# Backward input-gradient product: most x rows ride in the memory rows' column groups, the rest once per four segments

## The chip, the cores and the metric

The kernel runs on one core of one Trainium2 chip. The metric is the time of one execution in microseconds (us) on the device. Each ratio below is made among executions that took turns on the same chip. The times of the backward chain, the waits and the clocks are read from one profiled execution of each kernel, and not all of these ran on the same chip; the changed kernel was profiled twice, on two chips, and its chain took 1388.1 and 1385.1 us. Ratios and profiles here are of executions in the state "fast".

Names of engines in the profile: PE is TensorE (matrix products), PEld its weight loads, DVE is VectorE, ACT is ScalarE, POOL is GpSimd, SP is SyncE (here it only issues DMAs). A name with a q at its end (SPq, ACTq) is the time in that engine's instruction queue. "PEclk" is the clock that the chip granted to TensorE, as a share of full speed.

## The reference, cut to what matters

One transformer-like block with a recurrent memory, and its gradients. The sequence of 2048 rows is cut into 64 segments of 32 rows. Each segment attends to its own 32 rows and to 8 memory rows, and the 8 memory rows that leave it enter the next one:

```python
for s in range(n_seg):                      # 64 segments, one after the other
    xs = x[:, s * seg_len:(s + 1) * seg_len, :]
    h = jnp.concatenate([mem, xs], axis=1)  # 8 memory rows + 32 x rows = 40
    q, k, v = h @ Wq, h @ Wk, h @ Wv        # 16 heads of 256 = 4096 columns; the model is 448 wide
    p = softmax(where(mask, q @ k.T * scale, -1e9))
    o = (p @ v) @ Wo
    mem = o[:, :M, :]                       # goes into the next segment
    outs.append(o[:, M:, :])
# ... around it: layer norm, residual, a gated feed-forward block
_out, _vjp = jax.vjp(_f, A_x, A_mem0, A_Wq, ...)
_grads = _vjp(grad_out)
```

The gradient runs through the segments in the opposite order: segment s needs the gradient of its outgoing memory from segment s + 1. This chain of 64 dependent steps can't be parallelised.

## The kernel before

The program has a forward part and the feed-forward block (to about 1810 us), the backward chain of 64 segments (1810 to 3051 us) and a tail with the weight gradients and the x gradient (to 3886 us). One step of the backward chain, cut:

```python
for s in range(NSEG - 1, -1, -1):
    t, r = divmod(s, 4)                      # group of four segments, place in it (3, 2, 1, 0)
    ...
    with k.prio.crit():
        pss = [k.ps1() for _ in range(3)]
        for j in range(MC):                  # MC = 32: the Wo product, 128 matmuls -> doT
            ...
        for b in range(3):
            c0, n, v = c12(pss[b], b)
            k.evac(doT[:, c0:c0 + n, 0:L], v, "vsv"[b])        # PSUM -> SBUF on DVE (v) or ACT (s)
        nc.sync.dma_start_transpose(out=dO_sb, in_=doT...)     # "the doT transfer": v needs it
        pD = k.ps1()
        ...                                  # softmax backward on DVE -> dS_bd; 16 transposes on PE -> dST_bd
        for wi, (nm, lhs, rhs, WT) in enumerate((("k", Q_sb, dS_bd, WkT_sb), ("v", dO_sb, P_bd, WvT_sb),
                                                 ("q", K_sb, dST_bd, WqT_sb))):
            pp = [k.ps1() for _ in range(3)]
            head_mm(pp, lhs, rhs)            # 16 matmuls
            for b in range(3):               # first the 8 memory rows, small evictions
                c0, n, v = c12(pp[b], b)
                k.evac(d8[nm][:, c0:c0 + n, :], v[:, :, SEG:L], "vsv"[b])
            for b in range(3):               # then the 32 x rows, into the block of the group
                c0, n, v = c12(pp[b], b)
                k.evac(blk[nm][:, c0:c0 + n, r * SEG:(r + 1) * SEG], v[:, :, 0:SEG], "svs"[b])
            for j in range(MC):              # gradient of the memory rows: 8 wide, four column groups
                nc.tensor.matmul(pH[32 * (j % 4):32 * (j % 4) + M, 0:D], lhsT=d8[nm][:, j, :], rhs=WT[:, cj(j), :], ...)
        nc.vector.tensor_copy(out=om[:, 0:224], in_=pH[:, 0:224])        # "the omb copy"
        ...                                  # fp32 products with sel add up the four groups -> do_roll of segment s - 1
    ...
    if r == 0:                               # once per four segments, not in the critical chain
        px = k.fx1()
        for wi, (nm, WT) in enumerate((("k", WkT_sb), ("v", WvT_sb), ("q", WqT_sb))):
            for j in range(MC):              # gradient of 128 x rows: 96 matmuls, full width
                nc.tensor.matmul(px[:, 0:D], lhsT=blk[nm][:, j, :], rhs=WT[:, cj(j), :], ...)
            nc.gpsimd.dma_start(out=dr["X_" + nm][t], in_=blk[nm]...)    # 1 MB each: "the X writes"
        ...
```

A scheduler orders the instructions of each engine. What stands in the block of critical priority goes first; the 96 full-width products of a group, "the x products", fill what is left.

## Time and profile before

| | |
|---|---|
| time, median of three runs | 3879.49 us (3871.59 to 3894.95) |
| until the first omb copy | 1810.1 us |
| backward chain, first to last omb copy | 1241.3 us, PEclk 0.95 |
| tail | 835.0 us |
| mean segment in the chain, r = 3 / 2 / 1 / 0 | 23.7 / 18.5 / 17.9 / 19.0 us |

The segment times are the distances of the omb copies in the timeline of DVE, sorted by the place r of the segment in its group of four. The chain runs down, so r = 3 is the first segment after a group's end, when the three X writes are under way; it is called the boundary segment below.

The first part of the profile's page gives the busy time of each engine with its share of the span, here of the kernel before:

```profile
PE 3278.9 (84%) x54326; PEld 2060.7 (53%) x54326; DVE 1366.1 (35%) x3034; ACT 811.9 (21%) x1893; POOL 597.4 (15%) x1253
```

The view by windows cuts the span, here at the first and the last omb copy: the backward chain, then the tail. Its header names the columns.

```profile
core 0: us, PE busy (x) PEld busy (x) DVE busy (x) ACT busy (x) POOL busy (x), PEclk, DMA share, GB/s
1810.10:3051.39 1241.29, 1118.92 (x22044) 716.70 (x22045) 468.48 (x1198) 269.46 (x770) 251.41 (x559) 0.95 0.84 168
3051.39:3886.40 835.01, 718.32 (x3839) 331.63 (x3837) 129.61 (x265) 95.99 (x138) 58.68 (x79) 0.93 0.69 171
```

PE is 90% busy in the chain (1118.9 of 1241.3 us), but that doesn't yet say that its work is what the chain waits for. The chain of waits does: it is followed back from the last instruction, and each line is a start, a duration and what ran or was waited for. One plain segment of the kernel before (arA, arB and arW are three areas of SBUF, the on-chip memory that holds the operands; psf, po and fx are tiles in PSUM, to which the products are written and from which an "eviction" copies them to SBUF; psf L724 is the Wo product, psf L703 are the head products, po L765 the memory rows' products):

```profile
2147.64 3.33 PE psf L724 x128
...
2151.55 4.62 DMA arA<-arA
...
2156.21 0.32 PE psf L703 x4
2156.52 1.62 PE po L765 x32
2158.14 0.54 PE psf L703 x12
2158.68 1.68 PE po L765 x32
```

The longest link of the segment is no product: it is the transfer of doT, 4.62 us. The k branch does not need it. Its softmax backward, head products and evictions ran during the transfer and are not on the chain. Only its 32 memory-row products, the first x32, still follow the transfer, because in PE's queue they stand behind the first 4 head products of v.

Where do the x products run? The groups view (line, engine, operation, output<-input, shape and count; then busy us and mean ns; then idle time before) has their sum, and the timeline of PE (start, duration, count) their places:

```profile
L792 PE MATMUL fx<-arW,arA 128*128 128x448 bf16 x1536 | 370.6, 366 | 13.8 <-issue 13.8
L765 PE MATMUL po<-arW,arB 128*8 128x448 bf16 x6144 | 345.2, 368 | 19.9 <-DMA arW<-in_A_Wv_dram 11.1
```

```profile
2151.91 2.44 PE L792 MATMUL fx<-arW,arA 128*128 128x448 bf16 x12
...
2162.65 0.74 PE L792 MATMUL fx<-arW,arA 128*128 128x448 bf16 x3
...
3053.17 28.93 PE L792 MATMUL fx<-arW,arA 128*128 128x448 bf16 x152
```

Twelve run in the wait for the transfer (2151.55 to 2156.17), some more in the wait for the omb copies at the end of the segment, and 152 are left over when the chain has ended. They come one per 190 ns (28.93 us for 152), while 32 of the 8-wide ones on four column groups take 1.62 to 1.68 us, 52 ns each. That agrees with the Trainium skill, "TensorE: Matmul & The Clock Gate", Part 3: products whose outputs lie in different column groups run in the array at the same time.

### The profile page before, as it was taken

To read this page: it belongs to the slowest core of one execution; us is meant where nothing else is said; L and a number is where in the kernel's file an instruction comes from. 1 tells how busy PE (TensorE), PEld (TensorE's weight loads), DVE (VectorE), ACT (ScalarE), POOL (GpSimd) and SP (SyncE) were. 2 spreads that over 40 slices of the span, in tenths; PEclk is the share of its full clock that TensorE was granted. 3 is DMA by queue.
4 is the path that set the end of the run, shared out by engine and by line. 5 is a ranking of instruction groups with operands and counts; after the bars stand their busy time and mean duration, and the time that the engine had idled before them with its cause. 6 is when DMAs were issued, how large, how long until landed. Compare 5 with 4: busy or idle time off the path is not lost.

```text
span 3886.4 us, 120434 instructions
## 1 busy us (share of the span) xinstructions
PE 3278.9 (84%) x54326; PEld 2060.7 (53%) x54326; DVE 1366.1 (35%) x3034; ACT 811.9 (21%) x1893; POOL 597.4 (15%) x1253
## 2 busy tenths in 40 slices
PE   3888898899888668864898898899999967888899
PEld 2666666666665445643555555556556533333444
DVE  3443344334333346652333343334333232101101
ACT  1222222222222122321221222122222101111200
POOL 3111111111111111121221122112222111000000
PEclk9999999999998789986998999999999988999999
DMA  7444544554544677799798888878888978788652
GB/s 251 143 148 146 174 150 151 162 163 144 168 145 146 167 167 182 180 216 199 167 189 149 158 166 169 165 159 167 177 187 164 306 207 171 142 153 161 163 184 70
DMA packets 1156246, 658.10 MB, mean 169 GB/s; under 512 B 1045268, under 2 KB 1075780, under 8 KB 1148180
## 3 DMA queue, kind: packets, MB, share of 16 engines
q1 hardware_dynamic: 1068100, 392.72, 49.1%
q0 software_dynamic: 60272, 234.11, 17.8%
q10 hardware_dynamic: 27360, 23.58, 2.1%
q8 instruction: 425, 6.96, 0.8%
q14 instruction: 89, 0.73, 0.1%
HBM read 120.04 MB, written 268.02 MB: 100 GB/s over the span
## 4 chain that ended last, share of the span: by engine, by line
PE 64%; DMA 19%; issue 5%; DVE 4%; SPq 4%; ACT 3%; POOL 1%; ACTq 0%; DVEq 0%; POOLq 0%
PE psf L381 11%; DMA arA<-arA 10%; PE po L765 8%; PE psf L875 7%; PE psf L724 5%; PE fx L792 5%; PE po L465 4%; PE psf L703 3%; PE psf L562 2%; PE psf L422 2%; PE fx L494 2%; PE fx L362 2%; PE fx L880 2%; ACT arA L77 2%; PE psf L474 1%
## 5 line engine op out<-in xcount | busy, mean ns | idle before, releaser
L75 DVE CAST arA<-psf 128x480 bf16<-128x480 f32 (+4 forms) x709 | 403.1, 575 | 936.7 <-PE psf L381 323.5
L77 ACT CAST arA<-psf 128x384 bf16<-128x384 f32 (+4 forms) x883 | 404.8, 489 | 1325.5 <-PE psf L381 343.4
L381 PEld LDWEIGHTS <-arW 128*128 128x128 bf16 x16384 | 437.4, 98 | 32.4 <-issue 20.6
L381 PE MATMUL psf<-arA,arW 128*128 128x40 bf16 x16384 | 439.4, 182 | 17.2 <-issue 11.6
L792 PE MATMUL fx<-arW,arA 128*128 128x448 bf16 x1536 | 370.6, 366 | 13.8 <-issue 13.8
L75 DVE CAST arB<-psf 128x96 bf16<-128x96 f32 (+2 forms) x640 | 179.4, 287 | 525.7 <-PE psf L703 284.7
L765 PE MATMUL po<-arW,arB 128*8 128x448 bf16 x6144 | 345.2, 368 | 19.9 <-DMA arW<-in_A_Wv_dram 11.1
L77 ACT CAST arB<-psf 128x96 bf16<-128x96 f32 (+1 forms) x384 | 115.2, 300 | 735.7 <-PE psf L703 566.7
L875 PE MATMUL psf<-arW,arA 128*128 128x512 bf16 x990 | 260.1, 391 | 9.7 <-ACT arA L77 9.7
L724 PE MATMUL psf<-arA,arW 128*128 128x40 bf16 x8192 | 220.4, 180 | 49.7 <-POOL arA L671 38.4
L724 PEld LDWEIGHTS <-arW 128*128 128x128 bf16 x8192 | 219.1, 96 | 69.7 <-issue 55.5
L875 PEld LDWEIGHTS <-arA 128*128 128x128 bf16 x1440 | 138.5, 101 | 212.3 <-issue 73.9
L562 PE MATMUL psf<-arA,arW 128*128 128x256 bf16 x1344 | 167.3, 287 | 79.2 <-DMA arA<-arA 39.1
L765 PEld LDWEIGHTS <-arB 128*8 128x8 bf16 x6144 | 135.8, 88 | 161.3 <-issue 39.2
L792 PEld LDWEIGHTS <-arA 128*128 128x128 bf16 x1536 | 143.5, 106 | 135.6 <-issue 53.0
L562 PEld LDWEIGHTS <-arW 128*128 128x128 bf16 x1344 | 138.1, 103 | 110.6 <-issue 84.7
L362 PE MATMUL fx<-arW,arA 128*128 128x512 bf16 x512 | 136.0, 387 | 52.9 <-DMA arA<-XN 39.4
L422 PE MATMUL psf<-arW,arB 128*32 128x512 bf16 x2048 | 151.1, 387 | 1.8 <-issue 1.8
L465 PE MATMUL po<-arW,arB 128*8 128x448 bf16 x2048 | 146.2, 441 | 2.9 <-DVE arB L75 0.3
L896 PE MATMUL psf<-arW 128*128 128x448 bf16 x450 | 98.8, 371 | 38.8 <-DVE arA L75 38.8
L456 PE MATMUL psf<-arB,arA 128*128 128x80 bf16 x1024 | 53.4, 211 | 90.3 <-DMA arA<-arA 74.6
L703 PE MATMUL psf<-arB,arA 128*128 128x80 bf16 x1024 | 61.4, 212 | 70.3 <-DMA arA<-arA 70.0
(344 smaller groups left out, 3788.9 us busy)
## 6 DMA issues: line engine op xcount, KB each, us to landing
QT<-arA POOLq DMA_DIRECT2D x64, 512.0 KB, 4.0
KT<-arA SPq DMA_DIRECT2D x64, 512.0 KB
VG<-arA SPq DMA_DIRECT2D x64, 512.0 KB
X_o<-arA POOLq DMA_DIRECT2D x40, 512.0 KB, 4.4
Vx<-arA POOLq DMA_DIRECT2D x32, 512.0 KB, 3.3
arA<-Vx SPq DMA_DIRECT2D x128, 128.0 KB
X_k<-arA POOLq DMA_DIRECT2D x16, 1024.0 KB, 7.9
X_v<-arA POOLq DMA_DIRECT2D x16, 1024.0 KB, 8.3
```

The costliest lines, as they stand in the source:

```text
L75: nc.vector.tensor_copy(out=out, in_=in_)
L77: nc.scalar.copy(out=out, in_=in_)
L362: nc.tensor.matmul(pv[:, 0:512], lhsT=hx_b[t % 2][:, kc, :], rhs=Wv_sb[:, kc, n * 512:(n + 1) * 512], start=(kc == 0), stop=(kc == KC - 1))
L381: nc.tensor.matmul(pss[b][:, jj * L:(jj + 1) * L], lhsT=W_sb[:, kc, c * P:(c + 1) * P], rhs=hT_roll[:, kc, sl, :], start=(kc == 0), stop=( ...
L422: nc.tensor.matmul(pV[b][32 * j:32 * j + 32, 0:512], lhsT=memT_pad[:, kc, :], rhs=Wv_sb[:, kc, n * 512:(n + 1) * 512], start=(kc == 0), st ...
L465: nc.tensor.matmul(pO[32 * (j % 4):32 * (j % 4) + M, 0:D], lhsT=o8[:, j, :], rhs=Wo_sb[:, cj(j), :], start=(j < 4), stop=(j >= MC - 4), sk ...
L562: nc.tensor.matmul(ps[:, f2 * 256:(f2 + 1) * 256], lhsT=Wt[:, kc, c * P:(c + 1) * P], rhs=xT[:, kc, :], start=(kc == 0), stop=(kc == KC - 1))
L703: nc.tensor.matmul(ps[b][:, i * 2 * L:(i + 1) * 2 * L], lhsT=lhs[:, cl, :], rhs=rhs_bd[:, cl // 2, :, :].rearrange("p g n -> p (g n)"), st ...
L724: nc.tensor.matmul(pss[b][:, jj * L:(jj + 1) * L], lhsT=WoT_sb[:, kc, c * P:(c + 1) * P], rhs=do_roll[:, kc, sl, :], start=(kc == 0), stop ...
L765: nc.tensor.matmul(pH[32 * (j % 4):32 * (j % 4) + M, 0:D], lhsT=d8[nm][:, j, :], rhs=WT[:, cj(j), :], start=(wi == 0 and j < 4), stop=(wi ...
L792: nc.tensor.matmul(px[:, 0:D], lhsT=blk[nm][:, j, :], rhs=WT[:, cj(j), :], start=(wi == 0 and j == 0), stop=(wi == 2 and j == MC - 1))
L875: nc.tensor.matmul(pa[2 * kc + g][:, 0:w], lhsT=lhs_of(b)[:, kc * P:(kc + 1) * P], rhs=rhs_of(b, g), start=(b == 0), stop=(b == nblk - 1), ...
```

## The change

Its intent: 1536 full-width x products leave the kernel. The memory rows' products use 8 columns of a column group that could take 32, at no more streaming time. So the 40 rows of a segment are put in another order, and 24 of the 32 x rows ride with the 8 memory rows in the same product. Only 8 x rows per segment are left. They are collected over four segments and go, 32 columns in four column groups, through 96 packed products per group. The diff, cut to its core:

```diff
-            pss = [k.ps1() for _ in range(3)]
+            pss = [k.ps1() for _ in range(4)]
 ...
-            nc.sync.dma_start_transpose(out=dO_sb, in_=doT.rearrange("p c n -> p (c n)"))
+            for hf in range(2):                        # two half transposes
+                nc.sync.dma_start_transpose(out=dO_sb[:, 8 * hf:8 * hf + 8, :],
+                                            in_=doT[:, 16 * hf:16 * hf + 16, :].rearrange("p c n -> p (c n)"))
 ... softmax backward: scale fused in, one multiplication into dS_bd instead of two
-            for wi, (nm, lhs, rhs, WT) in enumerate((("k", Q_sb, dS_bd, WkT_sb), ("v", dO_sb, P_bd, WvT_sb),
+            pH = k.po1()
+            for wi, (nm, lhs, rhs, WT) in enumerate((("v", dO_sb, P_bd, WvT_sb), ("k", Q_sb, dS_bd, WkT_sb),
                                                      ("q", K_sb, dST_bd, WqT_sb))):
+                if nm == "k":                          # the 16 transposes into dST_bd now stand here
 ...
                 for b in range(3):
                     c0, n, v = c12(pp[b], b)
-                    k.evac(d8[nm][:, c0:c0 + n, :], v[:, :, SEG:L], "vsv"[b])
+                    k.evac(blk[nm][:, c0:c0 + n, r * SEG:(r + 1) * SEG], v[:, :, M:L], "vsv"[b])
                 for b in range(3):
                     c0, n, v = c12(pp[b], b)
-                    k.evac(blk[nm][:, c0:c0 + n, r * SEG:(r + 1) * SEG], v[:, :, 0:SEG], "svs"[b])
+                    k.evac(lo[nm][:, c0:c0 + n, r * M:(r + 1) * M], v[:, :, 0:M], "svs"[b])
                 for j in range(MC):
-                    nc.tensor.matmul(pH[32 * (j % 4):32 * (j % 4) + M, 0:D], lhsT=d8[nm][:, j, :], ...
+                    nc.tensor.matmul(pH[32 * (j % 4):32 * (j % 4) + 32, 0:D],
+                                     lhsT=blk[nm][:, j, r * SEG:(r + 1) * SEG], ...
 ...
-        for nm in "kvq":
-            nc.gpsimd.dma_start(out=dr["M_" + nm][s], in_=d8[nm]...)
         if r == 0:
+            for nm in "kqv":                           # X and M written once per group
 ...
                 for j in range(MC):
-                    nc.tensor.matmul(px[:, 0:D], lhsT=blk[nm][:, j, :], ...
+                    nc.tensor.matmul(px[32 * (j % 4):32 * (j % 4) + 32, 0:D], lhsT=lo[nm][:, j, :], ...
 ... the sums of the column groups and a transpose put the rows together again; the tail loads rows in the new order
```

So the change is four things at once: packing, with the work that puts the rows together again; v before k; two half transposes, four eviction banks and a shorter softmax backward; fewer and larger writes of the memory rows.

## The prediction

> **What bounds it now.** The table by stage puts the backward chain at about 1810 to 3030 us, the tail at 3030 to 3886. By starts of the omb copy (DVE timeline) 64 segments take about 19.4 us each: some 18.2 us inside a group of four, 24.0 us on average for the segment that crosses a group boundary. The chain of waits in a plain segment: Wo product 3.3 us, last eviction 0.5, transpose DMA of doT 4.3 to 5.4, then 6.5 us of TensorE work that needs it, then 2.3 us of omb copies, fp32 selection and cast. At boundaries the DMA takes 6.5 to 8 us (3 MB of X writes in flight), sometimes with 4 to 5 us of "issue" stalls.
>
> The 1536 full-width products that the change removes (groups: 370.6 us busy) run one per 0.19 us: 18.2 us per group, 290 us in all. But the timeline shows them as filler: of 21 in a plain segment, 12 or 13 sit in the doT transfer, 7 in the omb chain. Little of them is on the chain, except a backlog: after the last segment 152 run in a row, 28.9 us, ahead of the tail.
>
> **Added.** 1536 products of 32 columns in four column groups. The existing ones of that kind take 1.65 us per 32 (52 ns each), as the Trainium skill, "TensorE: Matmul & The Clock Gate", Part 3, says of column packing; the trace agrees (52 against 190 ns). So 80 us return: PE work falls by about 200 us net. Widening the memory rows' products from 8 to 32 columns costs nothing in streaming, but they now wait for a 384-column eviction (0.55 us) rather than 96 (0.25): +0.3 us, three times a segment.
>
> **Moved.** doT goes in two half transposes: estimated from issue (1.2 us for a quarter size, 1.95 for full) plus 2.5 us, halves land 6.3 and 7.9 us after the segment's start, against 8.4. But v now comes first, and VectorE's order puts the first v eviction between the reduction and the last softmax-backward steps, so the k branch, which hid in the transfer, now follows it: about 11.5 us from first half to next segment. Estimate 17.8 us against 18.2; boundaries 22.5 against 24. Backward: about -45 us.
>
> Tail: backlog 28.9 to about 6 us, moving the row-by-row layer-norm loop (8 us per step, VectorE queue blocks the evictions) some 20 us earlier; an extra load per step +5; memory-row loads in 1 KB instead of 256 B pieces (now 5.5 to 7.6 us each, on the chain) -15. Risk: without filler PE idles about 2 us per segment and the granted clock (0.93 to 0.98 there) may fall: +15.
>
> **Prediction:** 3815 us, 8 in 10 between 3735 and 3880. Faster by over 2%: 0.42; within 2%: 0.53; slower: 0.05.
>
> **Shown right by:** PE busy down 150 to 250 us, span down by only a third; plain segments 17.3 to 18.2 us; PE's waits for the doT transfer up from 70 us; transfer still first or second on the chain of waits; the tail starting its products within 10 us of the last segment. **Wrong if** plain segments are under 17 us (the split lands earlier, or the filler did cost), boundaries drop below 21 us, or the clock falls under 0.9.
>
> **What would make it wrong:** halves landing within 3 us; M writes (three small ones per segment, now one batch per group) having slowed the transposes more than I think; single-buffered blocks making v evictions wait for X writes (slack estimated at 14 us against 8 to 14 us landing) would cost.

## The result, and the profile after

The changed kernel took 4027.62 us (4018.29 to 4034.69). The kernel before took 3887.22 us beside it. The ratio is 1.0353, with a 95% interval of 1.0288 to 1.0417: slower by 3.5%. The ratios here and below are made from fast runs of the same rounds, so they are not quite the ratio of the medians that are quoted. The prediction had said 3815 us, at most 3880. Each group of experiments ran on one chip, which differed between groups, and the kernel before ran in each: its fast runs there have medians of 3904, 3902 and 3889 us. Ratios are therefore compared, rather than times.

| us | before | after | change |
|---|---|---|---|
| until the first omb copy | 1810.1 | 1807.6 | -2.5 |
| backward chain | 1241.3 | 1388.1 | +146.8 |
| tail | 835.0 | 827.4 | -7.6 |
| mean segment r = 3 | 23.7 | 26.4 | +2.7 |
| r = 2 | 18.5 | 22.7 | +4.2 |
| r = 1 | 17.9 | 19.7 | +1.8 |
| r = 0 | 19.0 | 19.6 | +0.6 |

All of the loss lies in the chain, and it is largest in the second segment of a group. Busy times and windows of the changed kernel, as before:

```profile
PE 3250.6 (81%) x54460; PEld 2063.5 (51%) x54526; DVE 1366.3 (34%) x2969; ACT 840.1 (21%) x2053; POOL 524.2 (13%) x1129
```

```profile
1807.59:3195.68 1388.09, 1112.13 (x22292) 722.96 (x22293) 472.45 (x1135) 296.92 (x927) 177.97 (x418) 0.83 0.75 150
3195.68:4023.10 827.42, 700.32 (x3788) 322.03 (x3790) 129.54 (x265) 96.39 (x140) 57.97 (x95) 0.92 0.69 176
```

PE's busy time in the chain has hardly moved (1118.9 to 1112.1 us), although 1536 full-width products have become packed ones. The clock has: 0.95 to 0.83. The records that make up this mean show only 1.00 and 0.50, so 0.83 means about 34% of the chain at half clock, 0.95 about 10%. The Trainium skill, "TensorE: Matmul & The Clock Gate", Part 1, names the same two states, half and full, and a window of about 3.4 us after which the chip changes between them. The trace agrees: the records of the clock in the chain last 3.41 us or a multiple of it.

The groups answer to those shown above:

```profile
L775 PE MATMUL po<-arW,arA 128*32 128x448 bf16 x6144 | 442.6, 410 | 44.8 <-DVE arA L75 34.9
L806 PE MATMUL fx<-arW,arA 128*32 128x448 bf16 x1536 | 142.2, 396 | 0.0
L711 PE MATMUL psf<-arB,arA 128*128 128x80 bf16 x1024 | 79.5, 243 | 194.6 <-DMA arA<-arA 194.3
```

The x products did shrink (370.6 to 142.2 us). But the memory rows' products got slower on average (368 to 410 ns), and the head products L711 now have 194.3 us of waiting for the doT transfer before them; the page of before has 70.0 there. In the view of PE's waits, limited to 1830 to 3030 us (what waits for what: us in total, times, longest), the same wait before and after:

```profile
PE psf L703 <- DMA arA<-arA: 66.1, 45, 7.7
```

```profile
PE psf L711 <- DMA arA<-arA: 155.0, 72, 17.5
```

The chain of waits of a plain segment after (psf L732 is the Wo product, psf L711 the head products, psf L761 the transposes of dS, po L775 the memory rows' products, DVE arB L75 the eviction of dS's transposes, DVE arA L75 that of k):

```profile
2023.86 3.40 PE psf L732 x128
...
2027.78 3.28 DMA arA<-arA
...
2031.10 0.72 PE psf L711 x8
2031.81 0.49 PE po L775 x3
2032.31 0.25 PE psf L761 x5
2032.56 1.93 PE po L775 x19
2034.50 0.22 PE psf L761 x8
...
2034.74 0.48 DVE arB L75
2035.22 0.48 DVE arA L75
...
2035.74 1.70 PE po L775 x32
2037.44 0.68 PE psf L711 x16
...
2038.61 1.51 PE po L775 x32
```

The second half of doT lands 7.2 us after the segment's start (2023.86 to the head products' start at 2031.10); before, the whole landed after 8.6 us (2147.64 to 2156.21). So the split works. But v's products, the transposes of dS and then k's all follow it now. In the segment after, the boundary, the transfer's link is 6.82 us instead of 3.28:

```profile
2046.52 6.82 DMA arA<-arA
```

And the clock falls in the middle of the plain segment. Three windows of the changed kernel; the last columns are PEclk, DMA share and GB/s:

```profile
2027.00:2030.50 3.50, 1.72 (x57) 1.27 (x54) 1.84 (x4) 0.67 (x2) 1.54 (x5) 1.00 0.80 149
2030.50:2034.00 3.50, 3.40 (x48) 1.51 (x40) 1.51 (x4) 0.69 (x2) 1.45 (x3) 0.56 1.15 101
2034.00:2038.00 4.00, 3.63 (x80) 2.17 (x72) 1.64 (x5) 1.25 (x4) 1.08 (x2) 0.96 1.08 365
```

The corresponding stretch of the kernel before, the wait for doT with its filler:

```profile
2136.00:2139.50 3.50, 2.29 (x47) 1.46 (x49) 1.83 (x6) 1.58 (x5) 1.61 (x3) 1.00 1.23 162
```

With filler, 65% of 3.5 us were busy and the clock stayed at full speed. Without it, 49% were busy, and half clock followed just when the products of the critical chain came: 1.93 us for 19 of them, while 32 take 1.70 us at full clock. No single gap of PE was long in that stretch; the longest in the timeline is this one (idle time before, in brackets):

```profile
2029.22 0.46 PE L711 MATMUL psf<-arB,arA 128*128 128x80 bf16 x8 [1.11 <-DMA arA<-arA]
```

No rule for the clock follows from these two stretches. Two other windows, both cut where the clock's own records begin and end, say the opposite. The first is of the kernel before, 49% busy, and full clock followed; the second of the changed kernel, 77% busy, and half clock followed:

```profile
1935.46:1938.88 3.42, 1.66 (x36) 0.87 (x36) 0.52 (x2) 1.13 (x3) 1.07 (x2) 1.00 0.98 170
2263.00:2266.42 3.42, 2.62 (x55) 1.93 (x44) 0.58 (x2) 0.58 (x2) 0.21 (x1) 1.00 0.80 198
```

So the traces show the clock over the whole chain falling with the filler, and not what decides it in one window.

### Two theories

- **Order.** v first puts the k branch behind the doT transfer. The old order hid k's softmax backward, eviction and products in it. Rival to the clock.
- **Clock.** The x products were free, and more than free: they kept the clock full. Without them the remaining products run at half clock for a third of the chain.

### The profile page after: what moved, and what is told of

It reads as the page before. It is cut to its first block, busy times and chain, and to the rows that moved or that the text cites. A ratio compares the mean times of both kernels' runs of the same rounds, so it can differ in the third digit from the quotient of the medians.

```text
span 4023.1 us, 120689 instructions
## 1 busy us (share of the span) xinstructions
PE 3250.6 (81%) x54460; PEld 2063.5 (51%) x54526; DVE 1366.3 (34%) x2969; ACT 840.1 (21%) x2053; POOL 524.2 (13%) x1129
## 3 DMA queue, kind: packets, MB, share of 16 engines
q0 software_dynamic: 58976, 238.56, 16.9%
## 4 chain that ended last, share of the span: by engine, by line
PE 63%; DMA 19%; DVE 5%; issue 5%; SPq 4%; ACT 3%; POOL 1%; ACTq 0%; DVEq 0%; POOLq 0%
PE psf L382 11%; DMA arA<-arA 10%; PE po L775 10%; PE psf L899 7%; PE psf L732 4%; PE po L466 4%; PE psf L711 3%; PE fx L806 2%; PE psf L423 2%; ACT arA L77 2%; PE psf L569 2%; PE fx L495 2%; PE psf L782 2%; PE fx L904 2%; PE fx L363 2%
## 5 line engine op out<-in xcount | busy, mean ns | idle before, releaser
L75 DVE CAST arA<-psf 128x320 bf16<-128x320 f32 (+6 forms) x1093 | 498.5, 481 | 1246.7 <-PE psf L711 346.9
L77 ACT CAST arA<-psf 128x480 bf16<-128x480 f32 (+6 forms) x1139 | 442.8, 407 | 1883.8 <-PE psf L711 383.5
L775 PE MATMUL po<-arW,arA 128*32 128x448 bf16 x6144 | 442.6, 410 | 44.8 <-DVE arA L75 34.9
L382 PEld LDWEIGHTS <-arW 128*128 128x128 bf16 x16384 | 438.3, 98 | 30.8 <-issue 18.6
L732 PE MATMUL psf<-arA,arW 128*128 128x40 bf16 x8192 | 227.3, 183 | 62.2 <-POOL arA L680 37.8
L775 PEld LDWEIGHTS <-arA 128*32 128x32 bf16 x6144 | 163.0, 105 | 202.0 <-DVE arA L75 64.2
L732 PEld LDWEIGHTS <-arW 128*128 128x128 bf16 x8192 | 225.8, 98 | 77.4 <-issue 72.5
L899 PEld LDWEIGHTS <-arA 128*128 128x128 bf16 x1440 | 138.5, 100 | 206.8 <-issue 66.3
L711 PE MATMUL psf<-arB,arA 128*128 128x80 bf16 x1024 | 79.5, 243 | 194.6 <-DMA arA<-arA 194.3
L75 DVE CAST arB<-psf 40x320 bf16<-40x320 f32 (+2 forms) x256 | 92.4, 361 | 310.5 <-PE psf L457 145.9
L569 PEld LDWEIGHTS <-arW 128*128 128x128 bf16 x1344 | 138.3, 103 | 106.4 <-issue 80.6
L711 PEld LDWEIGHTS <-arA 128*128 128x128 bf16 x1024 | 58.5, 123 | 254.6 <-DMA arA<-arA 232.1
L920 PE MATMUL psf<-arW 128*128 128x448 bf16 x450 | 103.0, 382 | 64.0 <-DVE arA L75 53.8
L466 PE MATMUL po<-arW,arB 128*8 128x448 bf16 x2048 | 149.0, 448 | 2.8 <-DVE arB L75 0.3
L806 PE MATMUL fx<-arW,arA 128*32 128x448 bf16 x1536 | 142.2, 396 | 0.0
L920 PEld LDWEIGHTS <-arW 128*128 128x128 bf16 x606 | 61.8, 103 | 129.8 <-issue 70.9
L457 PE MATMUL psf<-arB,arA 128*128 128x80 bf16 x1024 | 56.1, 217 | 89.3 <-DMA arA<-arA 73.8
```

The source lines that it names most:

```text
L75: nc.vector.tensor_copy(out=out, in_=in_)
L77: nc.scalar.copy(out=out, in_=in_)
L382: nc.tensor.matmul(pss[b][:, jj * L:(jj + 1) * L], lhsT=W_sb[:, kc, c * P:(c + 1) * P], rhs=hT_roll[:, kc, sl, :], start=(kc == 0), stop=( ...
L466: nc.tensor.matmul(pO[32 * (j % 4):32 * (j % 4) + M, 0:D], lhsT=o8[:, j, :], rhs=Wo_sb[:, cj(j), :], start=(j < 4), stop=(j >= MC - 4), sk ...
L569: nc.tensor.matmul(ps[:, f2 * 256:(f2 + 1) * 256], lhsT=Wt[:, kc, c * P:(c + 1) * P], rhs=xT[:, kc, :], start=(kc == 0), stop=(kc == KC - 1))
L711: nc.tensor.matmul(ps[b][:, i * 2 * L:(i + 1) * 2 * L], lhsT=lhs[:, cl, :], rhs=rhs_bd[:, cl // 2, :, :].rearrange("p g n -> p (g n)"), st ...
```

## The experiments

### Only the filler taken away: b_nofill

The kernel before with 6 of the 96 x products of a group; its x gradient is wrong (the comparison's tolerance did not notice). Neither order nor transfer changes.

```diff
-                for j in range(MC):
+                for j in (0, MC - 1):
                     nc.tensor.matmul(px[:, 0:D], lhsT=blk[nm][:, j, :], rhs=WT[:, cj(j), :],
```

> Kernel before with 90 of the 96 full-width x products per group dropped (out_1 wrong on purpose), nothing else moved. Clock theory (the products filled idle time and kept the TensorE clock granted): backward clock falls from 0.95 to 0.83-0.88, plain segments rise from 18.2 to 19.5-21 us, backward +60 to +150 us, tail -25, total +30 to +120 us although 270 us of products are gone. Order theory (v first puts k behind the transfer; filler harmless): clock effect small, plain segments stay 18.0-18.3 us, total -25 to -50 us.

Measured: 3958.54 us, ratio 1.0153 (1.009 to 1.0217). A kernel that does less and nothing else differently is slower. Its window of the backward chain:

```profile
1812.94:3113.47 1300.53, 1007.54 (x20755) 681.65 (x20756) 471.55 (x1197) 266.92 (x771) 251.95 (x560) 0.79 0.77 160
```

The chain is 59 us longer at a clock of 0.79, though PE is busy for 111 us less in it. PE's wait for the doT transfer, 60.4 us, is no longer than before (66.1); what has grown is its wait for dS (4.9 to 143.2 us, from 1830 to 3030 us), in the stretch that the filler had filled. This loss can't come from the order; it comes with the clock. Two numbers of the forecast were missed: the clock fell lower than 0.83, and the tail became 4 us shorter, not 25.

### Only filler put back: a_warm

The changed kernel with 8 useless full-width products per segment, in the two places where PE waits. They write a PSUM tile that the real products start anew.

```diff
+            pH = k.po1()
+            def keep_warm(n):
+                for _ in range(n):
+                    nc.tensor.matmul(pH[:, 0:D], lhsT=WoT_sb[:, 0, 0:P], rhs=WoT_sb[:, 1, 0:D], start=True, stop=True, ...)
+            keep_warm(5)                       # after the products of pD
 ...                                            # and keep_warm(3) in the middle of v's head products
-            pH = k.po1()
```

> Changed kernel plus 8 useless 448-column products per segment, in the two waits around the first half of v. Clock theory: backward clock back to 0.92 or more, total 60 to 110 us below the changed kernel (3920-3970 us) though it does more work. Order theory: same as the changed kernel or up to 20 us slower.

Measured: 3940.13 us, ratio 1.0127 (1.0047 to 1.0208), against 1.0353 without. Its window of the chain:

```profile
1811.43:3109.42 1297.99, 1098.69 (x22796) 705.14 (x22797) 468.01 (x1135) 295.84 (x927) 176.94 (x418) 0.93 0.79 160
```

512 useless products shorten the chain by 90 us (1388.1 to 1298.0) and bring the clock to 0.93. The memory rows' products are back to 367 ns in the mean: their width of 32 columns costs nothing, as predicted, when the clock is full. The wait for doT is still 155.8 us, the chain still 57 us longer than before. So the clock explains a good part, and not all. By place in the group (r = 3 / 2 / 1 / 0) the mean segments are 26.7 / 18.7 / 19.2 / 18.3 us, against 26.4 / 22.7 / 19.7 / 19.6 without: the second segment is back to that of before (18.5), the boundary segment gains nothing.

### A control with the same instructions, but hardly any work: a_tiny

The same 8 products, 16 columns wide instead of 448.

```diff
-                    nc.tensor.matmul(pH[:, 0:D], lhsT=WoT_sb[:, 0, 0:P], rhs=WoT_sb[:, 1, 0:D], start=True, stop=True,
+                    nc.tensor.matmul(pH[:, 0:16], lhsT=WoT_sb[:, 0, 0:P], rhs=WoT_sb[:, 1, 0:16], start=True, stop=True,
```

> Control for the useless products: the same 8 per segment, but 16 columns wide instead of 448, so the order and the waits change as there but TensorE gets nearly no extra busy time. Clock theory: no gain, within 25 us of the changed kernel, backward clock 0.82-0.85. If it was the order of instructions: about 90 us faster, as with wide ones.

Measured: 4004.91 us, ratio 1.0235 (1.0167 to 1.0303); chain 1336.4 us at a clock of 0.86. As a control of the total it fails: it lies between the changed kernel and a_warm in the clock and in the time, where narrow products should have given next to nothing. Sorted by place it says more. Its mean segments r = 3 / 2 / 1 / 0 are 25.7 / 19.5 / 20.2 / 19.8 us, of which 9.1 / 1.1 / 7.3 / 6.4 us ran at half clock; those of the changed kernel are 26.4 / 22.7 / 19.7 / 19.6 us, with 9.6 / 8.1 / 6.8 / 6.0. The gain lies in the second segments (16 times 3.2 us), the one place where the clock came back, and PE's wait for doT is no shorter there (1.9 us a segment against 1.6). That is what the clock theory says, though the order of the other instructions there was not compared. Why these few products brought the clock back there, and only there, is open.

### Only the order: a_kfirst

```diff
-            for wi, (nm, lhs, rhs, WT) in enumerate((("v", dO_sb, P_bd, WvT_sb), ("k", Q_sb, dS_bd, WkT_sb),
+            for wi, (nm, lhs, rhs, WT) in enumerate((("k", Q_sb, dS_bd, WkT_sb), ("v", dO_sb, P_bd, WvT_sb),
```

> Changed kernel with the branches in the old order k, v, q. Order theory: 80 us or more faster than the changed kernel (below 3945 us). Clock theory: TensorE still idles about 2.5 us per segment before dS is there, clock stays 0.82-0.88, total within 40 us of the changed kernel.

Measured: 3895.8 us, ratio 0.9992 (0.9928 to 1.0055). The chain is 1247.2 us, 141 us shorter than after the change, as the order theory had said and against the clock theory's limit. PE's wait for doT falls to a fraction of 155.0 us:

```profile
PE psf L711 <- DMA arA<-arA: 19.6, 10, 7.2
```

The clock is still only 0.88. With the k branch in the wait, PE has something to do there; the two causes therefore overlap, and their gains can't be added (141 and 90 us are more than the loss of 147).

### The rest of the change without the packing: b_tweaks and b_halves_fuse

Both keep the x products of the kernel before, and so the filler. b_tweaks takes four eviction banks with two half transposes, the fused softmax backward, and v first. b_halves_fuse takes the same but leaves the order k, v, q. They differ only in the order:

```diff
-            for wi, (nm, lhs, rhs, WT) in enumerate((("k", Q_sb, dS_bd, WkT_sb), ("v", dO_sb, P_bd, WvT_sb),
+            for wi, (nm, lhs, rhs, WT) in enumerate((("v", dO_sb, P_bd, WvT_sb), ("k", Q_sb, dS_bd, WkT_sb),
 ...                                   # and the 16 transposes of dS_bd move behind v
```

> Kernel before with the other parts of the change (v first, two half transposes, fused dS) but the old x products as filler. Clock theory: clock 0.93 or more, total within 1.5% of before. Order theory: 100 us or more slower than before (over 2.5%).

> Kernel before with the half transposes and the fused dS, but the old order k, v, q and the old x products; differs from the earlier run with v first in the order alone. If v first is what cost: 80 to 110 us faster than that run, boundary segments back to 23-24 us, total within 1% of before or up to 1.5% faster. If the halves or the fused dS cost: stays 60 us or more above before.

Measured: b_tweaks 3998.05 us, ratio 1.0249 (1.0185 to 1.0314); b_halves_fuse 3867.16 us, ratio 0.9878 (0.9825 to 0.9931). The windows of the chain, first b_tweaks:

```profile
1817.83:3126.21 1308.38, 1136.04 (x22029) 697.21 (x22030) 444.86 (x1134) 295.48 (x833) 250.23 (x559) 0.94 0.78 159
```

Then b_halves_fuse:

```profile
1811.86:3005.46 1193.60, 1089.55 (x22034) 705.79 (x22035) 449.25 (x1134) 287.99 (x833) 251.50 (x559) 0.95 0.90 174
```

At nearly the same clock, 0.94 and 0.95, the order alone costs 115 us of the chain. This settles that the order is a cause of its own. (Neither forecast for the total of b_tweaks was met: it is more than the clock theory's 1.5% slower, and just under the 2.5% of the order theory.) The waits of PE for doT, in the same order of kernels:

```profile
PE psf L703 <- DMA arA<-arA: 139.7, 78, 9.6
```

```profile
PE psf L703 <- DMA arA<-arA: 26.7, 10, 5.9
```

And the chain of waits of a plain segment in b_halves_fuse has no transfer in it at all. It goes from the eviction through filler to the head products, and the transfer lands meanwhile:

```profile
2127.27 3.26 PE psf L724 x128
2130.59 0.43 ACT arA L77
2131.38 2.56 PE fx L792 x13
2134.32 0.82 PE psf L703 x20
2135.14 1.62 PE po L765 x32
```

Mean segments r = 3 / 2 / 1 / 0: b_tweaks 28.0 / 19.6 / 17.9 / 18.0 us, b_halves_fuse 24.3 / 18.9 / 16.5 / 16.5. The order costs most in the boundary segment, where the transfer is late. (Both have, beyond that, a longer tail than before, 868 and 857 against 835 us; that was not studied.)

### Order and filler together, packed: ak_warm8 and ak_warm8_g

The changed kernel, k first, with 8 useless full-width products after those of pD. ak_warm8_g has, in addition, a gate: three small products into v's PSUM banks that read k's last evicted block, so that the scheduler can't put v's head products, which wait for the transfer, ahead of k's 32.

```diff
+            keep_warm(8)                                         # both
 ...
+                if nm == "v":                                    # ak_warm8_g only
+                    for b in range(3):
+                        nc.tensor.matmul(pp[b][0:SEG, 0:D], lhsT=blk["k"][:, MC - 1, r * SEG:(r + 1) * SEG],
+                                         rhs=WoT_sb[:, 1, 0:D], start=True, stop=True, skip_group_check=True)
```

> Changed kernel with order k, v, q and 8 useless 448-column products per segment while dS is computed. If order and clock are separate costs that add up: backward clock 0.93 or more instead of 0.88, plain segments 17.3 us, total 30 to 60 us under the run with k first alone, 3840-3870 us, so 1 to 1.5% faster than before. If order alone mattered: no change to the run with k first.

> The previous one, and three small products that make v's head products wait for k's evictions, so that the 32 products of k run before v needs the transfer. If late transfers at the group boundary still cost there: boundary segments 1 to 2 us shorter than without, total 15 to 30 us less (3820-3850 us). If not: the same within 10 us.

Measured: ak_warm8 3878.97 us, ratio 0.9919 (0.9873 to 0.9965); ak_warm8_g 3832.48 us (median of its three fast runs; a fourth was slow, 3884.39), ratio 0.9779 (0.9708 to 0.985). Chains 1237.0 us at 0.94 and 1213.9 us at 0.96. With both causes undone the packed kernel is faster than the kernel before. That does not yet show that packing pays: b_halves_fuse, without it, has the shorter chain (1193.6 us), and the intervals of the two ratios overlap. ak_warm8 gained less than expected over a_kfirst: its plain segments are shorter (17.0, 17.5, 16.9 us against 17.8, 18.4, 18.6), but its boundary is longer, 27.8 us against 24.7, and PE waits 50.2 us for doT instead of 19.6. With the gate the boundary is 24.6 us and the wait 14.0 us, a larger gain than was expected. So the order of PE's queue decides there again, as the scheduler makes it.

### The boundary segment: b_hf_spread, b_hf_spread_g

What is left is the boundary: 24.3 us in b_halves_fuse against 16.5 to 18.9. Three X writes of 1 MB are issued together at the end of the segment before it, ahead of its doT transposes. b_hf_spread takes b_halves_fuse and issues one write in each of the three following segments, after that segment's doT has landed. A write of one element, which the full one overwrites, makes it wait for the landing. b_hf_spread_g has the gate on top.

```diff
             for hf in range(2):
                 nc.sync.dma_start_transpose(...)
+            if r > 0 and t + 1 < NT:
+                nm = {3: "k", 2: "v", 1: "q"}[r]
+                nc.gpsimd.dma_start(out=dr["X_" + nm][t + 1][0:1, 0:1], in_=dO_sb[0:1, 15, 0:1])
+                nc.gpsimd.dma_start(out=dr["X_" + nm][t + 1], in_=blk_b[nm][(t + 1) % 2].rearrange("p c n -> p (c n)"))
 ...
-                nc.gpsimd.dma_start(out=dr["X_" + nm][t], in_=blk[nm].rearrange("p c n -> p (c n)"))
+                if t == 0:
+                    nc.gpsimd.dma_start(out=dr["X_" + nm][t], in_=blk[nm].rearrange("p c n -> p (c n)"))
```

> Kernel before with half transposes and fused dS, and the three 1 MB X writes of a group no longer at its end but one in each of the next three segments, each held back until that segment's doT transfer has landed. If the X writes make the boundary segment long: its mean falls from 24 us to 17-20, the other segments rise by less than 1 us, total 40 to 100 us under the same kernel without the spread (ratio to before 0.965 to 0.978). If something else does (instruction fetch, the DHb load): boundary stays at 23 us or more, total within 15 us.

> The same plus three small products that keep v's head products behind k's evictions. If the late transfer still blocks k anywhere: 10 to 25 us faster than without. If the spread has taken that away: within 10 us.

Measured: b_hf_spread 3780.96 us (3773.76 to 3784.81), ratio 0.9681 (0.9611 to 0.9751): the best, faster than both kernels. Its chain and its wait for doT:

```profile
1824.91:2931.93 1107.02, 1069.51 (x22034) 699.93 (x22035) 449.31 (x1135) 288.29 (x833) 274.54 (x602) 0.98 0.94 188
```

```profile
PE psf L703 <- DMA arA<-arA: 6.9, 7, 2.6
```

The boundary segment falls from 24.3 to 16.5 us, the chain by 87 us, and the clock is 0.98. One part of the forecast was missed: the fourth segment (r = 0) rose from 16.5 to 18.1 us, not by less than 1. In the changed kernel the queue of SyncE shows the same collision: the issue of the two half transposes in a plain segment, then in a boundary segment with the X writes on their way, with what the queue issued just before:

```profile
2026.15 2.86 SPq L737 DMA_TRANSPOSE arA<-arA  x2
...
2038.15 8.27 SPq L685 DMA_TRANSPOSE arW<-KT  x1
2046.52 5.07 SPq L737 DMA_TRANSPOSE arA<-arA  x2
```

The Trainium skill, "Trainium Kernel Development and Optimization", Key Constraints, says that DMAs issued from the queues of SyncE, ScalarE and GpSimd run on the same 16 DMA engines and interleave. The writes are issued by GpSimd, the transposes by SyncE, and the transposes take 2.86 us to issue in the plain segment and 5.07 beside the writes.

A part of the delay stands before them. The load of KT, which the same queue issues first, also takes longer: in the 15 boundary segments of the changed kernel it takes 8.5 us in the mean to issue (2.2 to 2.6 in the others), and in 14 of them the first doT transpose is issued within 0.2 us of its end. In b_halves_fuse the load takes 7.5 us there, in b_hf_spread 2.3, and the first doT transpose is issued 3.2 us after the end of the Wo product in the one and 0.9 before it in the other. In the code only the q branch, the last, reads what this load brings. To issue it after the doT transposes was not tried.

The gate brought nothing here: 3807.12 us, ratio 0.976 (0.9666 to 0.9855), chain 1140.2 us. The intervals overlap; the medians are 26 us apart, more than was expected. PE's wait for doT was already down to 6.9 us, so there was little left for it to order; why the chain became longer was not studied.

### The changed kernel again: a_again

Unchanged, on the chip of the last group.

> The changed kernel again, on the same chip and in the same call as the best versions, for a ratio of the same rounds: 1.03 to 1.04 of before.

Measured: 4056.81 us, ratio 1.0394 (1.0311 to 1.0477); chain 1385.1 us at 0.82. The loss doesn't depend on the chip.

| kernel | ratio | chain, us | PEclk in it | wait for doT (1830 to 3030 us), us |
|---|---|---|---|---|
| before | 1 | 1241.3 | 0.95 | 66.1 |
| after | 1.0353 | 1388.1 | 0.83 | 155.0 |
| b_nofill: before without filler | 1.0153 | 1300.5 | 0.79 | 60.4 |
| a_warm: after with filler | 1.0127 | 1298.0 | 0.93 | 155.8 |
| a_kfirst: after in the old order | 0.9992 | 1247.2 | 0.88 | 19.6 |
| b_tweaks: before, halves, v first | 1.0249 | 1308.4 | 0.94 | 139.7 |
| b_halves_fuse: before, halves, k first | 0.9878 | 1193.6 | 0.95 | 26.7 |
| ak_warm8_g: after, old order, filler, gate | 0.9779 | 1213.9 | 0.96 | 14.0 |
| b_hf_spread: b_halves_fuse, X writes spread | 0.9681 | 1107.0 | 0.98 | 6.9 |

Four rows differ in two things, the order and the packing with all that belongs to it (b_halves_fuse, b_tweaks, a_kfirst, after). v first costs 115 us of the chain without packing and 141 with it; the packing costs 54 us in the old order and 80 with v first. The half transposes and the fused dS save 48 us (before against b_halves_fuse).

## Why the prediction was wrong

The time was wrong, and also the direction: 3815 us predicted, within 3735 to 3880, and 4027.62 measured. It gave a loss of over 2% a chance of 0.05.

Steps that held:

- The removed products were filler. b_nofill took 270 us of them away (90 of 96) and the chain got no shorter.
- Widening the packed products from 8 to 32 columns costs nothing in streaming: 368 ns before, 367 in a_warm.
- "the k branch, which hid in the transfer, now follows it": seen, with PE's waits for doT up from 66.1 to 155.0 us. The transfer stayed second on the chain of waits over the whole span (10%).
- The halves landed earlier than estimated, 5.4 and 7.2 us after the segment's start against 6.3 and 7.9.
- The tail starts its products 8.4 us after the last omb copy, before it was 30.5; the memory rows' loads take 4.9, 3.9 and 3.9 us instead of 7.6, 5.7 and 5.5.

Steps that failed (their sum, "Backward: about -45 us", measured +146.8):

- **"about 11.5 us from first half to next segment"**, so "17.8 us against 18.2". This term of the sum was too small. In the segment shown it took 13.3 us (2029.22 to 2042.54), though the half landed early, and the chain shown there has products at half clock and two evictions in it, of dS's transposes and of k. The mean r = 2 and r = 1 segments are 22.7 and 19.7 us. The step named the right mechanism, the k branch behind the transfer, but took its cost to be smaller than the gain of the split. b_tweaks against b_halves_fuse gives its cost, 115 us in the chain at nearly the same clock; before against b_halves_fuse gives the gain of the split with the fused dS, 48 us.
- **"boundaries 22.5 against 24"**. Where the transfer is late, everything behind it is late: 26.4 us for r = 3. The estimate took the plain segment's gain over to the segment in which the transfer is slowest, and in which SyncE's queue holds it behind the KT load.
- **"the granted clock (0.93 to 0.98 there) may fall: +15"**. The risk was named and sized too small. The clock went to 0.83. b_nofill puts its cost at 59 us of the chain net of the removed work; a_warm takes 90 us back, a_tiny 52 in the second segments. The prediction counted idle time per segment (2 us) and not what half clock then does to the products after it. Its own sign, "the clock falls under 0.9", came true.
- **"PE busy down 150 to 250 us"**: 28 us (3278.9 to 3250.6). The same products were counted at full clock; at half clock they are busy longer (the memory rows' products 442.6 instead of 345.2 us).
- **Tail**: about -30 us expected, -7.6 measured. The backlog went, 22.1 us of it, but other waits grew (these are the ones seen, not a full account): the loads of the x gradient's rows in the layer-norm loop went from 4.0 to 5.4 us, PE's waits behind DVE evictions in the o weights' row product from 38.8 to 53.8 us, and 8.4 us of waits for X_o loads appeared.

The prediction's own suspicion that evictions of v would wait for X writes did not come true: among the waits of DVE and ACT in the chain after the change there is none for an X write.

Open: why a_tiny got the clock back in the second segments; what the fewer writes of the memory rows did, which no run isolates; what the fp32 sums and transposes that put the rows together cost in the chain; stalls of PE called "issue", in which it waits for nothing that the profile shows (in b_halves_fuse 40.9 us in 8 places, the longest 11.5); the longer tails of b_tweaks and b_halves_fuse. A version that combines the packing, the old order, the gate and spread X writes was not tried: the packed kernel has one block per name where b_hf_spread has two.

## What to carry to other kernels

Before you remove work that is off the critical chain, ask what it does for the clock: in this chain, products that ran only in waits bought full clock for the products that counted, and their removal cost more than it gave. In a chain with one slow transfer, put every branch that does not need it between its start and its landing, in the order that the engines' queues really have, and price a new order in the segment where the transfer is slowest. When the transfer that a chain waits for and large writes share a step, try to move the writes behind its landing, and look at what stands before the transfer in its queue: here spreading the writes took 87 us off the chain.

## What the Trainium skill lacked or had wrong

- "TensorE: Matmul & The Clock Gate", the table "Why this matters for your kernels": it warns of PE-idle gaps over about 3 us. Here half clock also followed windows without such a gap: one of 3.5 us with PE 49% busy and a longest gap of 1.11 us, and one of 3.42 us with PE 77% busy. The page gives no busy share from which the clock stays full, and one window's share does not decide it here: after another window, 49% busy with a gap of 1.96 us, the clock stayed at 1.00.
- No page says that separate useless products in a wait can pay, or that removing useful ones from a wait can cost: 512 useless full-width products took 90 us off the chain (1388.1 to 1298.0 us), and leaving out 1440 useful ones added 59 us (1241.3 to 1300.5 us).
- "Trainium Kernel Development and Optimization", Key Constraints, says that DMAs from different queues interleave, but no page has a time for a short transpose beside large writes: two half transposes took 2.86 us to issue in a plain segment and 5.07 us beside X writes of 1 MB, and spreading the writes took the boundary segment from 24.3 to 16.5 us.
